# Attention products in 64-step blocks on quarters of TensorE, transposes in row halves, with waits through SyncE

## The chip, the cores and the metric

The kernel runs on one core of one Trainium2 chip. The metric is the device time of a launch in microseconds. Before the change three runs took 411.67, 411.74 and 412.81 us, with a median of 411.74 us.

## The reference

Two blocks follow each other. The first is linear attention with decay, for 4 batches, 8 heads, 768 steps and 48 numbers a head:

```python
for t in range(S):
    kt, vt, rt = (k[:, :, t], v[:, :, t], r[:, :, t])
    cur = np.einsum('bhd,bhe->bhde', u[None] * kt, vt)
    y[:, :, t] = np.einsum('bhd,bhde->bhe', rt, state + cur)
    state = w[None, :, :, None] * state + np.einsum('bhd,bhe->bhde', kt, vt)
```

So the output of step t takes in all earlier steps s < t, each decayed, and its own step s = t weighted with u instead. The second block is a mixture of eight experts over the 3072 rows of that output: a gate product gives logits, tokens are assigned greedily so that each expert has exactly 384, and each expert applies `relu(x @ w1) @ w2`. Everything is in 32-bit floats.

## The kernel before

The 768 steps are cut into 6 chunks of T = 128, and with 4 batches that gives 24 units, in the order of chunk and then batch. A unit holds all 8 heads, as 4 pairs a, with q = 0 or 1 for the head of a pair (j in the outputs). A head's 48 numbers lie in a field of PD = 64 partitions, so head q of a pair is on partitions 0 to 47 or 64 to 111.

The work of one unit n, with the names used below:

- `load(n)` (line 419) issues three transfers from SyncE's queue: kt, rt and vt of the unit, each 128 steps by 8 heads by 48 numbers, that is 1024 runs of 192 bytes. kt and rt have 6 buffers, vt has 8.
- `scale(n)` (line 432, VectorE) multiplies kt with powers of the decay into ks. `step_products(n)` (line 438, GpSimd) first calls `load(n + 4)` and then forms r*k*u, which `own(n)` (line 448, VectorE) sums into dd, one number per step and head.
- `rows_turned(n)` and `keys_turned(n)` (lines 456 and 468) transpose rt and ks on TensorE, four transposes of 128 by 128 each, into one bank of PSUM each. `receptances` (line 465, VectorE) and the copy of line 474 (ScalarE) bring them to rT and kT.
- `diagonal(n)` (line 451, ScalarE) writes eight matrices of 128 by 128 into AT, each the identity scaled with a head's dd.
- `pairs(n)` (line 517) forms the product of keys and receptances for each head, 8 matmuls, and VectorE copies it into AT where s < t (line 524), by a mask. AT[s, t] is then upper triangular with dd on its diagonal.
- `from_state(n)` (line 534), for all but the first chunk, and `outputs(n)` (line 560) add the share of the state and the share of AT into the same banks y_ps, and ScalarE copies them out (line 571). `new_state(n)` (line 543) forms the chunk's share of the state, for all but the last chunk.

The state and the outputs, y_ps, lie with their two halves of 64 columns on two halves of the partitions, so from_state already works in quarters of TensorE: 48 of 64 rows by 64 columns.

The loop over the units is at line 630. Iteration n transposes unit n + 2, loads unit n + 7 (through `step_products(n + 3)`), makes the pairs of n + 1 and the outputs of n. `logits` and `by_token` add the gate's logits of a chunk every fourth iteration. Pieces of the constants that the later search needs (`walk.constants`, line 755) are issued three to an iteration from iteration 3 on.

The order on every engine in the loop is written out by hand: two `manual_schedule` blocks (lines 620 and 621) hold TensorE, ScalarE, VectorE, GpSimd and SyncE to the order of the program. SyncE's queue has only the loads in the loop; it follows the program's order too, but it waits for other engines only where a buffer has to be free.

After the loop the attention's rows are transposed back, stored, and the search for the first expert's tokens runs (line 680). Then the experts follow (line 1439), bound by TensorE, with their weights on SyncE's queue.

## Time and profile before

| what | value |
|---|---|
| median of the runs | 411.74 us |
| the profiled execution | 412.36 us |
| its span, first to last instruction | 410.6 us |
| TensorE busy | 392.4 us, 96% |
| VectorE busy | 265.5 us, 65% |
| ScalarE busy | 148.3 us, 36% |
| GpSimd busy | 116.7 us, 28% |
| granted TensorE clock, mean | 0.998 |
| issue of a kt, rt, vt load to its landing, median | 4.6, 4.9, 4.9 us |
| ScalarE, one diagonal (line 454) | 391 ns, 192 times |
| VectorE, one masked copy of 512 elements (line 524) | 729 ns, 48 times |

PE is TensorE's matmuls and PEld its weight loads, DVE is VectorE, ACT is ScalarE, POOL is GpSimd and SPq is the queue of SyncE. L522 is line 522 of the kernel. A line of the timeline gives the start and the time from the first to the last end of a group of instructions, in us; the end of one group overlaps the start of the next, since matmuls are pipelined. A matmul in 32-bit floats shows as two records, a transpose as one.

### The profile page before, as it was taken

Reading aid. Unit: us, or ns where it says so; the run is one execution under the profiler, and the core shown is the slowest. Engines: PE = TensorE matmul, PEld = TensorE weight load, DVE = VectorE, ACT = ScalarE, POOL = GpSimd, SP = SyncE. Lnnn points to the kernel's source line nnn. Section 1 sums busy time; section 2 is a strip of 40 time slices with the busy share of each in tenths; the row PEclk is TensorE's granted clock in tenths of the full one; section 3 lists DMA queues with packets and bytes.
Section 4 is the critical chain, followed back from the end, with each engine's and each line's share of the span. In section 5 each row is a group of like instructions: output and inputs, shape, how many; then the busy total and the mean of one; then the engine's idle time right before and its main releaser. Section 6 shows DMA issues by size and latency. Waiting matters only on the chain. (4 is left out here: it accounts for less than half of the span.)

```text
span 410.6 us, 8511 instructions
## 1 busy us (share of the span) xinstructions
PE 392.4 (96%) x3174; PEld 289.7 (71%) x3174; DVE 265.5 (65%) x777; ACT 148.3 (36%) x382; POOL 116.7 (28%) x154
## 2 busy tenths in 40 slices
PE   7899999999987899989999999999999999999993
PEld 4688888888876585855785685595586577587583
DVE  5898879998568268478568658856856837421021
ACT  3898877878756021202112112121121211202200
POOL 5665965556200202210420320211112032201001
PEclk9999999999999999999999999999999999999999
DMA  9999999940029564712810730641461488201001
GB/s 146 166 169 175 176 161 173 176 81 2 3 96 335 176 231 160 228 38 63 294 68 5 277 121 23 208 178 39 172 214 40 142 306 285 57 21 38 0 21 38
DMA packets 93996, 54.43 MB, mean 133 GB/s; under 512 B 76784, under 2 KB 88176, under 8 KB 93936
## 3 DMA queue, kind: packets, MB, share of 16 engines
q1 hardware_dynamic: 89280, 41.70, 40.9%
q0 software_dynamic: 3072, 9.44, 6.9%
q10 hardware_dynamic: 1584, 2.56, 1.8%
q8 instruction: 29, 0.48, 0.5%
q14 instruction: 31, 0.25, 0.2%
HBM read 44.25 MB, written 9.44 MB: 131 GB/s over the span
## 5 line engine op out<-in xcount | busy, mean ns | idle before, releaser
L1328 PE MATMUL h_ps<-xT,w 128*128 128x384 f32 (+1 forms) x372 | 121.8, 475 | 0.0
L1328 PEld LDWEIGHTS h_ps<-xT,w 128*128 128x128 f32 x372 | 64.6, 190 | 35.9 <-issue 4.0
L1335 ACT ACTIVATE hid<-h_ps 128x384 f32<-128x384 f32 x56 | 27.5, 490 | 115.4 <-PE h_ps L1328 101.9
L1238 POOL DMA_INDIRECT xg<-x_rows,tok x24 | 25.0, 1040 | 144.0 <-issue 121.1
L454 ACT ACTIVATE AT<-ident,dd 128x128 f32<-128x128 f32 x192 | 59.4, 391 | 1.5 <-DVE dd L449 1.5
L1378 POOL DMA_INDIRECT out_dram<-o_sb,tok x24 | 25.9, 1078 | 106.1 <-DVE o_sb L1427 55.4
L1386 PE MATMUL o_ps<-w,hid 128*128 128x384 f32 x128 | 44.4, 493 | 0.9
L524 DVE COPY_PREDICATED AT<-mask,g_ps 128x512 f32<-128x512 uint8 x48 | 32.5, 729 | 7.2 <-PE g_ps L522 7.2
L1386 PEld LDWEIGHTS o_ps<-w,hid 128*128 128x128 f32 x128 | 23.5, 190 | 18.5 <-issue 4.4
L1407 PE MATMUL o_ps<-T,S 128*128 128x192 f32 x192 | 32.5, 326 | 0.0
L1407 PEld LDWEIGHTS o_ps<-T,S 128*128 128x128 f32 x192 | 31.4, 190 | 0.0
L522 PE MATMUL g_ps<-rT,kT 48*128 48x128 f32 x384 | 28.4, 285 | 0.1
L446 POOL TENSOR_TENSOR rk<-rk,u_bc 128x384 f32<-128x384 f32 x24 | 26.9, 1121 | 1.9
L445 POOL TENSOR_TENSOR rk<-rt,kt 128x384 f32<-128x384 f32 x24 | 24.8, 1034 | 9.0 <-DMA rt<-in_r_dram 7.0
L522 PEld LDWEIGHTS g_ps<-rT,kT 48*128 48x128 f32 x384 | 23.6, 187 | 4.9 <-issue 2.9
L567 PE MATMUL y_ps<-AT,vt 128*64 128x128 f32 x368 | 24.6, 276 | 0.0
L1407 PE MATMUL o_ps<-w,hid 128*128 128x192 f32 x128 | 24.6, 326 | 0.0
L1318 ACT COPY xT<-xT_ps 128x384 f32<-128x384 f32 x24 | 10.8, 481 | 34.2 <-PE xT_ps L1317 34.2
L1407 PEld LDWEIGHTS o_ps<-w,hid 128*128 128x128 f32 x128 | 20.9, 190 | 2.1
L1412 DVE TENSOR_TENSOR both<-o_ps,one 128x192 f32<-128x192 f32 x8 | 2.9, 358 | 27.7 <-ACT one L1418 27.7
L567 PEld LDWEIGHTS y_ps<-AT,vt 128*64 128x64 f32 x368 | 19.7, 137 | 0.9 <-issue 0.3
L466 DVE TENSOR_TENSOR rT<-rT_ps,wr 128x512 f32<-128x512 f32 x24 | 16.4, 683 | 5.3 <-PE rT_ps L461 5.2
(240 smaller groups left out, 593.1 us busy)
## 6 DMA issues: line engine op xcount, KB each, us to landing
w<-in_moe_w_dram SPq DMA_DIRECT2D x14, 1536.0 KB, 7.3
kt<-in_k_dram SPq DMA_DIRECT2D x24, 192.0 KB, 4.6
rt<-in_r_dram SPq DMA_DIRECT2D x24, 192.0 KB, 4.9
vt<-in_v_dram SPq DMA_DIRECT2D x24, 192.0 KB, 4.9
x_rows<-AT SPq DMA_DIRECT2D x8, 192.0 KB, 2.6
w<-in_moe_w_dram ACTq DMA_DIRECT2D x1, 1536.0 KB
x_rows<-rt SPq DMA_DIRECT2D x6, 192.0 KB, 3.4
x_rows<-ks SPq DMA_DIRECT2D x5, 192.0 KB, 2.8
```

Source lines behind the costliest of these rows:

```text
L445: nc.gpsimd.tensor_mul(rk, rt[:, :, 0:D], kt)
L446: nc.gpsimd.tensor_mul(rk, rk, self.u_bc.rearrange("p (h d) -> p h d", h=H))
L454: self.tc.nc.scalar.activation(AT[:, h % 2, h // 2, :], self.ident, AF.Copy, scale=dd[:, h:h + 1])
L522: nc.tensor.matmul(g_pss[q][:, a, :], kT[heads[q], a, :], rT[heads[q], a, :], start=True, stop=True)
L524: nc.vector.copy_predicated(out=AT[:, q], mask=mask.unsqueeze(1).to_broadcast([128, HP, T]), data=g_pss[q])
L567: nc.tensor.matmul(y[j][halves[i], g, :], vt[:, 2 * a + j, :], AT[:, j, a, :], start=(c == 0 and g == 0), stop=(g == 1), skip_group_check= ...
L1238: nc.gpsimd.indirect_dma_start(out=xg[:, c, :], out_offset=None, in_=x_dram, in_offset=bass.IndirectOffsetOnAxis(ap=tok[:, c:c + 1], axis=0))
L1328: product = nc.tensor.matmul(h_ps[:, cols], w1[:, f, ts(j, 128)], xT[:, f, cols], start=(f == 0), stop=(f == KD - 1))
L1335: nc.scalar.activation(hid[:, j, :], h_ps, AF.Relu)
L1378: nc.gpsimd.indirect_dma_start(out=out_rows[n * NC + c], out_offset=bass.IndirectOffsetOnAxis(ap=tok[:, c:c + 1], axis=0), in_=o_sb, in_of ...
L1386: nc.tensor.matmul(o_ps, hid[:, j, ts(c, 128)], w2[:, j, :], start=(j == 0), stop=(j == KF - 1))
L1407: nc.tensor.matmul(part, a[:, j, :], b[:, j, :], start=(j == 0), stop=(j == HF - 1))
```

## The change

Four parts, all but the last in the attention stage.

First, the products of pairs and outputs are cut into blocks of M = 64 steps. `pairs` makes two matmuls per head instead of one: block s = 0 against all 128 later steps, block s = 64 against the last 64 only. AT's rows 64 to 127 are stored with their columns moved to the left by 64, so that both diagonal blocks lie in columns 0 to 63: one masked copy serves both, and the block of rows 0 to 63 against steps 64 to 127 is copied whole by ScalarE (`across`). The diagonal matrices are 64 columns wide: five are made by ScalarE and three by one instruction of GpSimd. `outputs` takes the two row halves of AT and vt apart.

Second, the transposes of a unit are made in halves of 64 rows (`both_turned`): turn 0 takes rows 0 to 63 of rt and rows 64 to 127 of ks by turns, and turn 1 the other halves. In the same way outputs takes the heads j = turn for the first rows and the others for the last rows.

Third, [...] the first instructions of turn 1 wait until turn 0 has ended. `behind` makes that wait: a no-op on SyncE that waits for TensorE, and for which TensorE waits. The order of the loop changes with it: `scale` and `step_products` of n + 3, with the loads of n + 7, come first, pairs stands between the two turns of the transposes, and new_state between those of the outputs.

Fourth, eleven constants of the sure search (steps and top) are formed there and no longer ahead of it. The banks of PSUM in which the rows are turned at the end are three instead of four.

```diff
@@ -448,10 +453,14 @@
-    def diagonal(self, n, first=0, end=None):
+    def diagonal(self, n, part):
         AT, dd = self.live[n]["AT"], self.live[n]["dd"]
-        for h in range(first, end or self.r.shape[1]):
-            self.tc.nc.scalar.activation(AT[:, h % 2, h // 2, :], self.ident, AF.Copy, scale=dd[:, h:h + 1])
+        M, nc = T // 2, self.tc.nc
+        if part == 0:
+            nc.gpsimd.tensor_mul(AT[:, 1, 1:4, 0:M], self.own_step.unsqueeze(1).to_broadcast([128, 3, M]),
+                                 dd[:, 3::2].unsqueeze(2).to_broadcast([128, 3, M]))
+        for h in ((0, 1, 2), (4, 6))[part]:
+            nc.scalar.activation(AT[:, h % 2, h // 2, 0:M], self.own_step, AF.Copy, scale=dd[:, h:h + 1])
@@ -461,6 +470,32 @@
+    def behind(self, ins, other):
+
+        sync = mybir.DependencyInfo(mybir.DependencyClass.Sync, mybir.DependencyReason.DATA)
+        through = self.tc.nc.sync.nop().ins
+        self.tc.add_manual_dep(through, other.name, sync)
+        self.tc.add_manual_dep(ins, through.name, sync)
+
+    def both_turned(self, n, turn):
+
+        HP, live = self.r.shape[1] // 2, self.live[n]
+        names = ("rt", "rT_ps"), ("ks", "kT_ps")
+        if turn == 0:
+            for _, name in names:
+                live[name] = self.ps.tile([128, HP, T], F32, name=name)
+        for a in range(HP):
+            for i, (rows, into) in enumerate(names):
+                half = ts((turn + i) % 2, T // 2)
+                made = self.tc.nc.tensor.transpose(live[into][:, a, half],
+                                            live[rows][half, 2 * a:2 * a + 2, :].rearrange("p q d -> p (q d)"),
+                                            self.ident[half, half]).ins
+                if turn == 1 and a == 0:
+                    self.behind(made, live["half"])
+        live["half"] = made
+        if turn == 1:
+            self.tc.nc.scalar.copy(live["kT"], live.pop("kT_ps"))
@@ -518,10 +555,16 @@
         for a in range(HP):
-            for q in range(2):
-                nc.tensor.matmul(g_pss[q][:, a, :], kT[heads[q], a, :], rT[heads[q], a, :], start=True, stop=True)
-        for q in range(2):
-            nc.vector.copy_predicated(out=AT[:, q], mask=mask.unsqueeze(1).to_broadcast([128, HP, T]), data=g_pss[q])
+            for s in (0, M):
+                for q in range(2):
+                    nc.tensor.matmul(g_ps[s:s + M, q, a, 0:T - s], kT[heads[q], a, s:s + M], rT[heads[q], a, s:T],
+                                     start=True, stop=True)
+        for_all = mask.unsqueeze(1).unsqueeze(1).to_broadcast([128, 2, HP, M])
+        nc.vector.copy_predicated(out=AT[:, :, :, 0:M], mask=for_all, data=g_ps[:, :, :, 0:M])
+
+    def across(n):
+
+        nc.scalar.copy(live[n]["AT"][0:M, :, :, M:T], g_ps[0:M, :, :, M:T])
@@ -557,15 +600,24 @@
-        for g, j, i in order:
-            a = 2 * g + i
-            nc.tensor.matmul(y[j][halves[i], g, :], vt[:, 2 * a + j, :], AT[:, j, a, :],
-                             start=(c == 0 and g == 0), stop=(g == 1), skip_group_check=True)
+        for g in range(2):
+            for s in range(2):
+                j = (turn + s) % 2
+                for i in range(2):
+                    a, own = 2 * g + i, ts(s, M)
+                    made = nc.tensor.matmul(y[j][halves[i], g, s * M:T], vt[own, 2 * a + j, :], AT[own, j, a, 0:T - s * M],
+                                            start=(c == 0 and g == 0 and turn == 0), stop=(g == 1 and turn == 1),
+                                            skip_group_check=True).ins
+                    if turn == 1 and g == s == i == 0:
+                        mild.behind(made, live[n]["first"])
+        live[n]["first"] = made
+        if turn == 0:
+            return
@@ -625,29 +677,33 @@
             pairs(0)
-            mild.diagonal(1)
+            across(0)
+            for part in range(2):
+                mild.diagonal(1, part)
             mild.own(2)
             for n in range(N):
-                if n + 2 < N:
-                    mild.rows_turned(n + 2)
-                    mild.keys_turned(n + 2)
-                    mild.receptances(n + 2)
                 if n + 3 < N:
                     mild.scale(n + 3)
                     mild.step_products(n + 3)
                 if n + 2 < N:
-                    mild.diagonal(n + 2, 0, 4)
+                    mild.both_turned(n + 2, 0)
+                    mild.diagonal(n + 2, 0)
                 if n + 1 < N:
                     pairs(n + 1)
+                if n + 2 < N:
+                    mild.both_turned(n + 2, 1)
+                    mild.diagonal(n + 2, 1)
+                    mild.receptances(n + 2)
+                if n + 1 < N:
+                    across(n + 1)
                 if n > 0 and n % B == 0:
                     logits(n // B - 1)
-                if n + 2 < N:
-                    mild.diagonal(n + 2, 4)
                 from_state(n)
+                outputs(n, 0)
                 new_state(n)
                 if n > 0 and n % B == 0:
                     by_token(n // B - 1)
-                outputs(n)
+                outputs(n, 1)
@@ -662,7 +718,7 @@
-            banks += g_pss + [y_ps[:, 0], kv_ps]
+            banks += [g_ps[:, 0], kv_ps, y_ps[:, 0]]
```

More of the change, by code (lines that the diff above doesn't have):

```diff
@@ L343, in __init__ @@
         make_upper_triangular(nc, mask, val=1.0, diag=False)
-        self.mask = const.tile([128, 128], U8, name="mask")
-        nc.gpsimd.tensor_copy(self.mask, mask)
+        self.mask = const.tile([128, M], U8, name="mask")
+        self.own_step = const.tile([128, M], F32, name="own_step")
+        for i in range(2):
+            half = ts(i, M)
+            nc.gpsimd.tensor_copy(self.mask[half, :], mask[half, half])
+            nc.gpsimd.tensor_copy(self.own_step[half, :], ident[half, half])
         with part, tc.manual_schedule(engines={nc.tensor.engine, nc.vector.engine, nc.scalar.engine, nc.gpsimd.engine}):
@@ L408, in __init__ @@
             self.own(0)
-            self.diagonal(0, 0, 2)
+            self.diagonal(0, 0)
             self.keys_turned(0)
-            self.diagonal(0, 2)
+            self.diagonal(0, 1)
             self.step_products(1)
@@ L507, in attention_mild @@
     N = len(units)
+    M = T // 2
     lgT = {}
@@ L512, in attention_mild @@
     kv_ps = ps.tile([128, HP, T], F32, name="kv_ps")
-    g_pss = [ps.tile([128, HP, T], F32, name=f"g_ps{i}") for i in range(2)]
+    g_ps = ps.tile([128, 2, HP, T], F32, name="g_ps")
     last = []
@@ L558, in new_state, with outputs @@
                 nc.vector.tensor_mul(own, new, wc)
-    def outputs(n):
+    def outputs(n, turn):
         b, c = units[n]
@@ L564, in outputs @@
         y = banks_of(n)
-        for g, j, i in order:
-            a = 2 * g + i
-            nc.tensor.matmul(y[j][halves[i], g, :], vt[:, 2 * a + j, :], AT[:, j, a, :],
-                             start=(c == 0 and g == 0), stop=(g == 1), skip_group_check=True)
+        for g in range(2):
+            for s in range(2):
+                j = (turn + s) % 2
+                for i in range(2):
+                    a, own = 2 * g + i, ts(s, M)
[7 more added lines that the diff above has]
+            return
         into = turned[n].rearrange("p (g j) t -> p j g t", j=2)
@@ L676, in between @@
                 for _ in range(4):
-                    nc.tensor.matmul(g_pss[0][:, 0:3, :], ident, ident.unsqueeze(1).to_broadcast([128, 3, 128]),
+                    nc.tensor.matmul(g_ps[:, 0, 0:3, :], ident, ident.unsqueeze(1).to_broadcast([128, 3, 128]),
                                      start=True, stop=True)
@@ L743, in __init__ @@
         new("digits", [128, ND], I32)
-        new("steps", [128, 8, ND], I32)
-        new("top", [128, ND], I32)
         new("taken", [128, NT])
@@ L827, in constants @@
         nc.gpsimd.iota(self.digits, pattern=[[1, ND]], base=1, channel_multiplier=0)
-        yield
-        for g in range(8):
-            nc.vector.tensor_single_scalar(out=self.steps[:, g, :], in_=self.digits, scalar=28 - 4 * g,
-                                           op=ALU.logical_shift_left)
-            yield
-        nc.vector.tensor_single_scalar(out=self.top[:, 0:7], in_=self.steps[:, 0, 0:7], scalar=-1,
-                                       op=ALU.bitwise_xor)
-        yield
-        nc.vector.tensor_single_scalar(out=self.top[:, 7:ND - 1], in_=self.steps[:, 0, 7:ND - 1],
-                                       scalar=-2147483648, op=ALU.bitwise_xor)
-        yield
-        nc.vector.tensor_copy(self.top[:, ND - 1:ND], self.top[:, ND - 2:ND - 1])
         yield
@@ L1059, in surely @@
         tt(prop, self.by_expert(self.first_e), self.by_token(em), ALU.is_equal)
-        cand, bits = self.top, None
+        steps = pool.tile([128, 8, ND], I32, name="steps")
+        for g in range(8):
+            nc.vector.tensor_single_scalar(out=steps[:, g, :], in_=self.digits, scalar=28 - 4 * g,
+                                           op=ALU.logical_shift_left)
+        top = pool.tile([128, ND], I32, name="top")
+        nc.vector.tensor_single_scalar(out=top[:, 0:7], in_=steps[:, 0, 0:7], scalar=-1, op=ALU.bitwise_xor)
+        nc.vector.tensor_single_scalar(out=top[:, 7:ND - 1], in_=steps[:, 0, 7:ND - 1], scalar=-2147483648,
+                                       op=ALU.bitwise_xor)
+        nc.vector.tensor_copy(top[:, ND - 1:ND], top[:, ND - 2:ND - 1])
+        cand, bits = top, None
         for g in range(8):
@@ L1082, in surely @@
                 base = pool.tile([128, ND], I32, name="base")
-                tt(base, self.steps[:, g + 1, :], flip.to_broadcast([128, ND]), ALU.bitwise_xor)
+                tt(base, steps[:, g + 1, :], flip.to_broadcast([128, ND]), ALU.bitwise_xor)
                 cand = pool.tile([128, ND], I32, name="cand")
```

## The prediction

> **What bounds the kernel now.** First the busy shares: is one engine full?

> ```profile
> PE 392.4 (96%) x3174; PEld 289.7 (71%) x3174; DVE 265.5 (65%) x777; ACT 148.3 (36%) x382; POOL 116.7 (28%) x154
> ```

> TensorE is. The change touches only the attention stage, 16.4 to 115.7 us of the span, so the second view is TensorE's own timeline there: iteration 0 of the loop (line 630), then iteration 11.

> ```profile
> 16.44 0.66 PE L461 MATMUL rT_ps<-ident,rt 128*128 128x128 f32 x4
> 16.94 0.60 PE L472 MATMUL kT_ps<-ident,ks 128*128 128x128 f32 x4
> 17.47 1.71 PE L522 MATMUL g_ps<-rT,kT 48*128 48x128 f32 x16
> 19.11 0.56 PE L550 MATMUL kv_ps<-vt,ks 128*48 128x48 f32 x16
> 19.50 1.06 PE L567 MATMUL y_ps<-AT,vt 128*64 128x128 f32 x16
> 20.49 0.66 PE L461 MATMUL rT_ps<-ident,rt 128*128 128x128 f32 x4
> ...
> 62.49 0.66 PE L461 MATMUL rT_ps<-ident,rt 128*128 128x128 f32 x4
> 62.98 0.60 PE L472 MATMUL kT_ps<-ident,ks 128*128 128x128 f32 x4
> 63.51 1.16 PE L522 MATMUL g_ps<-rT,kT 48*128 48x128 f32 x16
> 64.60 0.67 PE L540 MATMUL y_ps<-rT,state 48*64 48x128 f32 x16
> 65.20 0.56 PE L550 MATMUL kv_ps<-vt,ks 128*48 128x48 f32 x16
> 65.60 1.06 PE L567 MATMUL y_ps<-AT,vt 128*64 128x128 f32 x16
> 66.59 0.66 PE L461 MATMUL rT_ps<-ident,rt 128*128 128x128 f32 x4
> ```

> Each group begins where the one before ends: a unit costs 66.59 - 62.49 = 4.10 us of TensorE (3.50 us for the first four, which have no state, line 540), and nothing else ends a wait. From start to start: transposes 1.02, pairs 1.09, from_state 0.60, kv 0.40, outputs 0.99.

> Third, the queue that the new waits go through. SyncE issues the loads of line 426 in program order; unit 7's are the last three before 28.99:

> ```profile
> 23.70 0.37 SPq L426 DMA_DIRECT2D kt<-in_k_dram  x1
> 24.23 0.46 SPq L426 DMA_DIRECT2D rt<-in_r_dram  x1
> 24.81 0.78 SPq L426 DMA_DIRECT2D vt<-in_v_dram  x1
> 25.77 0.84 SPq L426 DMA_DIRECT2D kt<-in_k_dram  x1
> 26.78 0.92 SPq L426 DMA_DIRECT2D rt<-in_r_dram  x1
> 27.81 1.00 SPq L426 DMA_DIRECT2D vt<-in_v_dram  x1
> 28.99 1.65 SPq L426 DMA_DIRECT2D kt<-in_k_dram  x1
> ```

> One issue holds SyncE for 0.4 to 2.7 us, one after the other, since the DMA engines are full there:

> ```profile
> DMA  9999999940029564712810730641461488201001
> ```

> By the program, unit 7 is loaded in iteration 0 (line 637 loads n + 3 + 4). TensorE began iteration 0 at 16.44; SyncE is done with that load at 28.81. SyncE is 12 us behind the program, and in the kernel before nobody minds, as iteration 0 itself needs only unit 3. The last load is issued at 84.5 and iteration 16 starts at 84.38: only there has TensorE come level.

> [...] within a mode a wave of records starts 0.109 us after the one before (two records in pairs and outputs, four 7 ns apart in from_state, line 540); at each change of mode the next group starts 0.20 us after the last record and its first wave takes 0.15 to 0.21. A change so costs (1.02 - 0.87) to (1.09 - 0.89), about 0.16 us. [...] The granted clock stays full 3.6 us past the last matmul (403.9), to 409.0, and averages 0.52 over 409.0 to 410.6; a pause within the kernel isn't shown.

> **The change, part by part,** per unit of TensorE.

> - *Pairs.* 8 products become 16 in four quarters. The column quarter of block s=0 still gets 4 heads x 2 records of 128 columns: 8 waves x 0.109 = 0.87 as now. The omitted block lay in the other quarter, which only idles sooner. I take 1.06 with one change of mode. Bounds: 1.31 + 0.16 if 64-column records don't overlap 128-column ones; 0.67 + 0.16 if the saved quarter of work shortens the group.
> - *Outputs.* The same: each row half s=0 does 4 products x 2 records of 128 columns, 2 x 4 waves x 0.109 = 0.87. Same two-sided bounds, +0.44 and -0.22.
> - *Transposes.* 8 waves of 128 columns become 8 waves of two halves with 64 columns, 2 x 4 x 0.055 = 0.44 in place of 0.87. No row has this form; the weight load of a transpose takes 140 ns where a 128-column product's takes 188, so loading shouldn't hold the wave. Bounds: 0.44, or 0.87 if it does.
> - *Modes.* Per unit turn 0, pairs, turn 1, from_state with outputs 0, kv, outputs 1: six changes for four, +0.32.
> - Sum with state: 0.38 + 1.06 + 0.38 + (0.436 + 0.436 + 0.16) + (0.36 + 0.16) + (0.436 + 0.16) = 3.97 for 4.10, **-0.13**, 16 units: -2.1. Without state 3.54 for 3.50: +0.2 for four. The last four have no kv between the two halves of outputs, so that wait is open (below): +0.25 in all after the modes saved.
> - *ScalarE* per unit: 2.44 us of diagonals becomes five of 64 columns plus a 512-element copy, some 1.3 + 0.58. *VectorE*: one predicated copy of 0.73 for two. *GpSimd*: one more of some 0.5 (a product of the same 192 elements, line 556, takes 0.507), to 2.8 in a unit of 3.97. All hidden under TensorE, which waits for none of them; if uncovered, at most GpSimd's 0.5 a unit. Moving the search's 11 constants: VectorE only, under the loop, 0; three more small GpSimd copies ahead of the loop fall into its idle 3.0 us before 6.83. Three banks for four at the end: rows' copies take 0.48 and their transposes 0.44, so 0.
> - *Waits through SyncE.* Turn 1's first transposes and the first product of outputs 1 wait for no-ops on SyncE. Queued behind them on TensorE is everything; behind them on SyncE, the loads of unit n + 8. Price with SyncE free: end of a record 0.27 after its start, hop 0.1 (kT's copy starts 0.09 after the transposes' end), 0.05, hop 0.1, so 0.52 after the last record. Outputs 1 has kv in front (start at +0.71): hidden; open without kv, +0.35. Turn 1 has pairs in front (+1.26): hidden.

> But SyncE isn't free. In iteration 0 the order there is: three issues of unit 7, then turn 1's no-op. Nothing lets those issues come earlier; they run against full DMA engines from 1.7 us on. So the no-op runs at 28.81 + 0.1, turn 1 at 29.05. Without the wait: 16.44 + 0.38, pairs from 17.4 (VectorE must free g_ps) to 18.5. **TensorE stands still for 10.5 us**, and iteration 1 starts at 29.05 + 0.38 + 0.60 + 0.52 + 0.60 = 31.15 for 20.49: **+10.7**.

> It isn't caught up: TensorE has no idle time later. [...] Later the no-op of outputs(n) releases unit n + 8's loads, and the next turn 1 waits for their issue. After outputs 0 ends, SyncE needs 0.2 + three issues of 1.7 (12.99 to 14.67[...]) to 1.9 + 0.15, about 2.2; TensorE has 0.52 + 0.60 + 0.38 + 1.06 less 0.07, 2.5, before it comes to turn 1. It just fits; in iterations 1 to 3 the DMA needs 3.4 a unit (24 in 82), +0.5 in all, and issues of up to 2.7 will sometimes stick out, **+1** (0 to 8).

> Sum: 10.7 + 1.7 + 0.2 + 0.5 - 2.1 + 0.25 + 1 = 12.2, rounded to **+12**: the span 410.6 becomes 422.6. That execution took 412.4, 0.6 above the median; laid on the median 411.74, **423.7 us**.

> **The rivals.**

> 1. *Stall, and TensorE dearer.* Mixed column counts don't overlap (+0.88 a unit), or half-row transposes save nothing (+0.43 on 22, +9.5), or SyncE sticks out by 0.5 on 16 units (+8). For: none of these forms is in the trace, and the vt issues reach 2.68. Against: from_state overlaps four. 429 to 445, about 433.
> 2. *The change does what it says:* products really get shorter by the missing quarter, 0.44 x 24 = -10.6. Against: the busy quarter keeps its columns. With the stall 413.1.
> 3. *No stall.* One mechanism: SyncE is at the first no-op when TensorE gets there, at 18.5 rather than 28.9. Then only the sums: -2.1 + 0.2 + 0.25 = -1.6, 410.1, faster. It decides once SyncE arrives before about 19.5 (stall under 1, no half clock). For: iteration 0 needs nothing of unit 7, so any other order of that queue gives it. Against: the queue is filled in program order, and its issues follow kt, rt, vt, unit by unit throughout.

> **How the numbers follow.** Main 0.52 (418 to 429), rival 1 0.25, rival 2 0.07, rival 3 0.16. Range 413 to 440: all of the main case, most of rival 1 and half of rival 2. Within 0.3% (1.2 us, what a measurement of this kernel can tell) are parts of rivals 2 and 3: faster 0.11, same 0.05, slower 0.84.

> **What would show it.** Right: a gap on TensorE before turn 1 in iteration 0, ended by SyncE near 29 us; then units of about 4.0; pairs still 1.06, transposes 0.38 per turn. Wrong: no such gap, or units of 3.5 or less (rival 2), or of 4.4 and more with turn 1 waiting for SyncE (rival 1). The forecast fails if the no-ops are queued ahead of the loads.

## The result, and the profile after

The changed kernel takes 429.41 us (median of 4 runs, 428.24 to 429.95) against 412.27 us (411.67 to 415.41) for the kernel before, run beside it. The ratio is 1.0396, with a 95% interval of 1.0338 to 1.0454: 17.1 us slower, where the forecast was 12 us slower (423.7 us, with a range of 413 to 440). The profiled execution took 429.95 us, its span is 428.2 us and its mean granted clock 0.959.

From the page of the changed kernel: the busy shares, the granted clock in 40 slices of 10.7 us, and a row of the costliest groups (busy time, mean ns of one, then the idle time before it and what ended it).

```profile
PE 398.8 (93%) x4118; PEld 291.6 (68%) x4118; DVE 245.3 (57%) x742; ACT 132.9 (31%) x334; POOL 130.7 (31%) x181
...
PEclk9955599999999999999999999999999999999999
...
L491 PE MATMUL rT_ps<-ident,rt 64*128 64x64 f32 x176 | 22.2, 253 | 9.1 <-SPq L477 9.1
```

TensorE is busy for 6.4 us more although it is given less to do: that is no sign of heavier work, since the clock row has three slices at half speed, from about 21 to 54 us. The third line has the idle time that was forecast: the first transposes of turn 1 (line 491) wait 9.1 us in all, and SyncE's no-op of line 477 ends all of it. TensorE's timeline of the same kernel shows where, in iteration 0:

```profile
16.62 1.09 PE L560 MATMUL g_ps<-rT,kT 48*64 48x128 f32 x32 [1.14 <-ACT AT L567]
...
26.37 0.36 PE L491 MATMUL rT_ps<-ident,rt 64*128 64x64 f32 x1 [8.66 <-SPq L477]
...
30.57 1.97 PE L560 MATMUL g_ps<-rT,kT 48*64 48x128 f32 x32
```

Pairs end at 17.71, turn 1 starts at 26.37, and in brackets stands the 8.66 us of idle time between. (The 1.14 us ahead of pairs are a wait for ScalarE's copy of line 567.) Before the gap a pairs group takes 1.09 us, after it 1.97. SyncE's own queue in that stretch:

```profile
25.64 0.63 SPq L431 DMA_DIRECT2D vt<-in_v_dram  x1
28.45 0.37 SPq L431 DMA_DIRECT2D kt<-in_k_dram  x1
```

The issue of unit 7's last transfer ends at 26.27, and turn 1 runs 0.10 us later. The next load is issued only from 28.45, after the second no-op of the iteration.

The busy time by stretches (PE, PEld, DVE, ACT, POOL, each with its count, then the granted clock, the DMA share and GB/s) has the second half of the story:

```profile
17.70:26.40 8.70, 0.04 (x3) 0.03 (x1) 0.73 (x1) 0.79 (x4) 3.21 (x4) 0.67 0.96 188
26.40:54.80 28.40, 28.40 (x456) 22.41 (x456) 11.02 (x21) 13.18 (x37) 9.12 (x13) 0.50 0.52 102
```

After the gap TensorE works for 28.4 us without a pause, and all that time at half its clock. In the clock's records the low stretch lies from 20.70 to 54.83. Then one unit, from the start of its pairs to the next one's, looks like this:

```profile
60.59 1.09 PE L560 MATMUL g_ps<-rT,kT 48*64 48x128 f32 x32
...
63.02 0.56 PE L593 MATMUL kv_ps<-vt,ks 128*48 128x48 f32 x16
63.52 0.65 PE L613 MATMUL y_ps<-AT,vt 64*64 64x128 f32 x16
...
64.50 1.09 PE L560 MATMUL g_ps<-rT,kT 48*64 48x128 f32 x32
```

A unit takes 64.50 - 60.59 = 3.91 us, where it took 4.10; kv, between the two halves of outputs, has 63.52 - 63.02 = 0.50. The 17 us by stretches of the two profiled executions, measured between starts of the kv products (lines 550 and 593) of the units named, and to the start of the search's most_ps product at the end of the stage:

| stretch | before | after | difference | what it is |
|---|---|---|---|---|
| start to unit 0 | 19.11 | 28.09 | +8.98 | gap 8.66; half clock 0.81; pairs' wait for ScalarE, less the earlier start of the loop (15.01 for 16.44), -0.5 |
| units 0 to 4 | 15.61 | 26.86 | +11.25 | half clock |
| units 4 to 19 | 66.08 | 63.41 | -2.67 | cheaper units, with one stop of 0.46 for SyncE |
| unit 19 to most_ps | 12.84 | 12.04 | -0.80 | last units |

The sum is +16.76, of 17.6 between the two spans. The same four units take 15.33 us in the next experiment, which keeps the full clock, so the half clock costs 26.86 - 15.33 = 11.53 there. From the end of the gap to the first kv product it is 28.09 - 26.37 = 1.72 us, where that experiment has 0.91 from the end of pairs: 0.81 more. Together that is **12.3 us**: more than the gap that set it off. (Texts below that were written before their runs say 12.5.)

### The profile page after: what moved, and what is told of

Read it like the earlier page. It is cut to its first block, busy times and chain, and to the rows that moved or that the text cites. A ratio compares the mean times of both kernels' runs of the same rounds, so it can differ in the third digit from the quotient of the medians.

```text
span 428.2 us, 10342 instructions
## 1 busy us (share of the span) xinstructions
PE 398.8 (93%) x4118; PEld 291.6 (68%) x4118; DVE 245.3 (57%) x742; ACT 132.9 (31%) x334; POOL 130.7 (31%) x181
## 5 line engine op out<-in xcount | busy, mean ns | idle before, releaser
L1438 PEld LDWEIGHTS o_ps<-w,hid 128*128 128x128 f32 x128 | 23.5, 190 | 18.5 <-issue 4.4
L463 ACT ACTIVATE AT<-own_step,dd 128x64 f32<-128x64 f32 x120 | 33.7, 342 | 1.5 <-DVE dd L454 1.5
L613 PE MATMUL y_ps<-AT,vt 64*64 64x128 f32 (+1 forms) x736 | 33.3, 274 | 0.3
L563 DVE COPY_PREDICATED AT<-mask,g_ps 128x512 f32<-128x512 uint8 x24 | 17.7, 738 | 23.0 <-PE g_ps L560 14.4
L560 PE MATMUL g_ps<-rT,kT 48*64 48x128 f32 (+1 forms) x768 | 29.7, 275 | 1.1 <-ACT AT L567 1.1
L491 PE MATMUL rT_ps<-ident,rt 64*128 64x64 f32 x176 | 22.2, 253 | 9.1 <-SPq L477 9.1
L491 PEld LDWEIGHTS rT_ps<-ident,rt 64*128 64x128 f32 x176 | 15.8, 152 | 18.2 <-SPq L477 10.4
L450 POOL TENSOR_TENSOR rk<-rt,kt 128x384 f32<-128x384 f32 x24 | 26.3, 1095 | 0.1
L560 PEld LDWEIGHTS g_ps<-rT,kT 48*64 48x64 f32 x768 | 23.3, 146 | 3.8 <-ACT AT L567 1.3
L613 PEld LDWEIGHTS y_ps<-AT,vt 64*64 64x64 f32 x736 | 22.9, 149 | 2.8 <-SPq L477 0.8
L491 PE MATMUL kT_ps<-ident,ks 64*128 64x64 f32 x176 | 22.2, 253 | 0.0
```

The lines of the kernel that those rows point to most:

```text
L450: nc.gpsimd.tensor_mul(rk, rt[:, :, 0:D], kt)
L463: nc.scalar.activation(AT[:, h % 2, h // 2, 0:M], self.own_step, AF.Copy, scale=dd[:, h:h + 1])
L491: made = self.tc.nc.tensor.transpose(live[into][:, a, half], live[rows][half, 2 * a:2 * a + 2, :].rearrange("p q d -> p (q d)"), self.iden ...
L560: nc.tensor.matmul(g_ps[s:s + M, q, a, 0:T - s], kT[heads[q], a, s:s + M], rT[heads[q], a, s:T], start=True, stop=True)
L613: made = nc.tensor.matmul(y[j][halves[i], g, s * M:T], vt[own, 2 * a + j, :], AT[own, j, a, 0:T - s * M], start=(c == 0 and g == 0 and tur ...
L1438: nc.tensor.matmul(o_ps, hid[:, j, ts(c, 128)], w2[:, j, :], start=(j == 0), stop=(j == KF - 1))
```

## The experiments

The theory after the result: SyncE's place in its queue makes the gap, the gap lowers the clock, and without a gap the change itself is a small gain. The rivals: the new forms keep the clock low by themselves; a gap on TensorE always costs that much; blocks or halves alone carry the loss or the gain.

**The waits through ScalarE.** ScalarE's queue has no loads. Its no-op stands right behind turn 0 and behind the first half of outputs, and what ScalarE does in between is put behind it.

```diff
-        through = self.tc.nc.sync.nop().ins
+        through = self.tc.nc.scalar.nop().ins
 ...
                     mild.both_turned(n + 2, 1)
-                    mild.diagonal(n + 2, 1)
                     mild.receptances(n + 2)
-                if n + 1 < N:
-                    across(n + 1)
 ...
                 outputs(n, 0)
+                if n + 2 < N:
+                    mild.diagonal(n + 2, 1)
+                if n + 1 < N:
+                    across(n + 1)
                 new_state(n)
```

> The changed kernel, with the same waits led through ScalarE instead of SyncE (two of ScalarE's steps move behind the wait of the outputs), so that no wait stands behind a load's issue. Theory (order of SyncE's queue, then the halved clock): the 8.7 us gap in iteration 0 and the half clock to 54.8 us both vanish; units stay at 3.9 us and 3.4 us without state; 429.4 - 8.7 - 12.5 = about 408, between 406 and 411. Rival (the quarter and half-row forms of the work are what costs): no less than 420, since they are all still there.

Measured: 408.35 us (three executions, 408.18 to 409.93) against 411.62, ratio 0.992 (0.99 to 0.9939). TensorE's timeline in iteration 0, and the stretch from 20 to 60 us:

```profile
18.09 1.09 PE L563 MATMUL g_ps<-rT,kT 48*64 48x128 f32 x32 [1.15 <-ACT AT L570]
...
21.56 1.09 PE L563 MATMUL g_ps<-rT,kT 48*64 48x128 f32 x32
```

```profile
20.00:60.00 40.00, 40.00 (x1136) 32.40 (x1136) 28.64 (x57) 29.92 (x83) 32.14 (x53) 1.00 0.93 184
```

From pairs to pairs it is 3.47 us, with no gap between, and the clock stays at 1.00. So in these executions the whole loss belongs to the queue that the waits go through: all the rest of the change is a gain of 3.3 us. The parts add up: 408.35 + 8.66 + 12.3 = 429.3, and 429.41 was measured. And in this trace the new forms don't lower a clock that is full.

A fourth execution took 420.42 us, at a mean granted clock of 0.963 where the three have 0.996 to 0.997. Its trace isn't kept. The 12 us and the mean clock are like those of the next experiment, where 27.3 us of half clock cost 11.6 us (mean clock 0.965). So this kernel may have lost the clock there too, with no load ahead of its waits; that isn't shown.

**The load moved nearer, waits still through SyncE.** In iteration 0 the no-op then stands behind unit 5's load and not unit 7's.

```diff
-        self.load(n + 4)
+        self.load(n + 2) if n > 1 else None
```

> The changed kernel with its waits on SyncE, but each load called two units later (n + 2 instead of n + 4), so that in iteration 0 the first wait stands behind unit 5's load and not unit 7's. Theory: the wait is reached when unit 5 is issued, 20.5 us in the changed kernel's trace, so the gap shrinks from 8.7 to about 2.9 us; [...] about 429.4 - 5.8 - 12.5 = 411, up to 416 if loads then come late. If the gap shrinks but the clock is halved all the same: about 423. Rival (forms of the work): 429, the gap being a by-product.

Measured: 423.64 us, ratio 1.0295 (1.0266 to 1.0323). TensorE's timeline and one stretch:

```profile
20.69 0.37 PE L491 MATMUL rT_ps<-ident,rt 64*128 64x64 f32 x1 [3.04 <-SPq L477]
```

```profile
36.00:48.00 12.00, 12.00 (x196) 9.30 (x194) 4.60 (x9) 5.95 (x17) 3.77 (x7) 0.50 0.51 100
```

The gap shrinks as expected, to 3.04 us, and 12 us are lost all the same, since even that gap halves the clock: it falls at 20.61 and comes back at 47.91. By the units at half clock (6.05 us for 3.47) these 27.3 us are worth an estimated 27.3 x (1 - 3.47 / 6.05) = 11.6. My belief that such a gap is just too short to count was wrong.

**The gap filled with work.** The no-op stays late, but 13 products of 128 x 384 run in the gap.

```diff
                     pairs(n + 1)
+                if n == 0:
+                    for _ in range(13):
+                        nc.tensor.matmul(kv_ps[:, 0:3, :], ident, ident.unsqueeze(1).to_broadcast([128, 3, 128]),
+                                         start=True, stop=True)
                 if n + 2 < N:
                     mild.both_turned(n + 2, 1)
```

> The changed kernel with 13 extra matmuls of 128x384 (8.5 us) on TensorE in iteration 0, ahead of the second turn of transposes, into a bank nobody reads: the wait stays as it is, but TensorE works through it. Theory (the clock falls to half in the gap and its slow recovery costs 12.5 us): the clock stays full, 429.4 - 12.5 = about 417, 415 to 419. Rival (time after the gap is set by SyncE and the loads, not by the clock): 426 to 430.

Measured: 420.6 us (418.91 to 423.18), ratio 1.0221 (1.0172 to 1.0271). The clock is full from 20 to 60 us, and its mean in the profiled execution is 0.996:

```profile
20.00:60.00 40.00, 38.39 (x874) 28.89 (x876) 20.62 (x42) 22.20 (x63) 23.28 (x39) 1.00 0.73 144
```

That is 429.41 - 420.6 = 8.8 us less than the changed kernel, with the wait still there. The time is above the 415 to 419 that were expected, for two reasons that its trace shows: the loop began 1.5 us later than in the changed kernel's execution, and TensorE's later stops for SyncE are 0.25, 0.96, 0.26 and 0.23 us, where the changed kernel has one of 0.46. With these 2.7 us counted in, the clock is worth an estimated 11.5 us by this road, against the 12.3 of the table.

**The kernel before with one such wait.** Nothing of the change but this: the first pair product of iteration 0 waits behind the load of unit 7.

```diff
+                if n == 1 and a == q == 0:
+                    sync = mybir.DependencyInfo(mybir.DependencyClass.Sync, mybir.DependencyReason.DATA)
+                    through = nc.sync.nop().ins
+                    tc.add_manual_dep(through, mild.turned_last.name, sync)
+                    tc.add_manual_dep(made.ins, through.name, sync)
```

> The kernel before with one wait of the same kind only: the first pair product of iteration 0 waits for a no-op on SyncE behind unit 7's load. Nothing else is changed. Theory: TensorE stands still from 17.5 to about 29, 11.4 us. If the clock then returns[...]: 412 + 11.4 + 1.7 = 425. If it stays half until the first logits, as in the changed kernel, four units of 3.5 and part of the fifth take double: 412 + 11.4 + 14 = 437. Rival (slow recovery is a trait of the new forms): 425.

Measured: 424.32 us, ratio 1.0312 (1.0287 to 1.0337). TensorE's timeline, then the stretches after the gap:

```profile
27.83 2.08 PE L522 MATMUL g_ps<-rT,kT 48*128 48x128 f32 x16 [9.93 <-SPq L525]
```

```profile
28.00:32.00 4.00, 4.00 (x46) 3.78 (x48) 2.02 (x4) 0.00 (x0) 0.00 (x0) 0.50 1.46 182
32.00:36.00 4.00, 4.00 (x52) 3.32 (x50) 1.73 (x4) 2.24 (x6) 2.01 (x2) 0.75 0.74 135
```

The gap is 1.3 us longer than in the changed kernel, but the full clock is back at 34.02, 6.2 us after work resumes. Half of 6.2 on top of 9.93 makes 13.0, and 12.7 were measured. A pause of 10 us does therefore not cost 28 us of half clock by itself: with the old forms the clock is back after 6. So in the changed kernel something in the new forms keeps it low.

**Which of the new forms?** One kernel has the half-row transposes alone and their wait through SyncE, the other the blocks alone, with whole transposes and the outputs' wait through SyncE.

```diff
 (the kernel before)
-                    mild.rows_turned(n + 2)
-                    mild.keys_turned(n + 2)
 ...
+                    mild.both_turned(n + 2, 0)
                     mild.diagonal(n + 2, 0, 4)
                 if n + 1 < N:
                     pairs(n + 1)
+                if n + 2 < N:
+                    mild.both_turned(n + 2, 1)
+                    mild.receptances(n + 2)
 (the kernel after)
-                    mild.both_turned(n + 2, 0)
+                    mild.rows_turned(n + 2)
+                    mild.keys_turned(n + 2)
+                    mild.receptances(n + 2)
 ...
-                    mild.both_turned(n + 2, 1)
                     mild.diagonal(n + 2, 1)
-                    mild.receptances(n + 2)
```

> The kernel before with the transposes alone changed (row halves in two turns, pairs between them, the wait through SyncE behind unit 7's load); pairs, outputs and diagonals as before. The gap in iteration 0 (about 9 us) and the fall of the clock are expected under every theory. What keeps the clock at half afterwards in the changed kernel? If the half-row transposes do: half until the first logits, 27 us after the gap and more, about 424 to 427. If the products in quarters do: full again within 7 us as in the kernel before with one wait, about 419 to 422.

> The changed kernel with whole transposes, as before the change; pairs and outputs in quarters, and the wait of the outputs through SyncE behind unit 7's load. A gap of about 7 us in iteration 0 under every theory. If the products in quarters keep the clock at half: half until the first logits near 55 us, about 428 to 432. If the half-row transposes do: full again within 7 us, about 420.

Measured, in two executions each: halves alone 418.64 us, ratio 1.0169 (1.0116 to 1.0223), blocks alone 419.01 us, ratio 1.0178 (1.0122 to 1.0234). The gaps are 9.3 and 5.7 us. Two stretches of the first, then the same of the second:

```profile
28.00:32.00 4.00, 3.77 (x50) 3.33 (x50) 1.98 (x4) 2.04 (x6) 1.25 (x1) 0.50 1.46 186
32.00:36.00 4.00, 3.53 (x74) 3.23 (x72) 2.67 (x6) 3.72 (x11) 1.00 (x1) 0.96 0.93 164
```

```profile
28.00:32.00 4.00, 4.00 (x87) 3.27 (x86) 2.12 (x5) 2.67 (x8) 0.00 (x0) 0.81 0.66 133
32.00:36.00 4.00, 4.00 (x94) 3.36 (x92) 3.07 (x7) 3.24 (x9) 3.09 (x4) 1.00 0.89 173
```

Neither keeps the clock low: it is back at 32.31 and 29.54, 4.1 and 4.0 us after work resumes. Both expectations had put the blame on one form or the other, and both fell. Only the two together, in the changed kernel and in the one with the load moved, stay at half clock, for 28.4 and 27.2 us of unbroken work. In both of these the first logits (128 x 32 products on all rows, 1.93 us) run just ahead of the return: they start at 51.23 and 45.56, and the clock is back at 54.83 and 47.91. The first from_state follows them (from 53.10 and 47.42).

**A burst right after the gap.** In the changed kernel seven products of 128 x 384 follow turn 1 in iteration 0.

```diff
+                if n == 0:
+                    for _ in range(7):
+                        nc.tensor.matmul(kv_ps[:, 0:3, :], ident, ident.unsqueeze(1).to_broadcast([128, 3, 128]),
+                                         start=True, stop=True)
                 if n > 0 and n % B == 0:
                     logits(n // B - 1)
```

> The changed kernel with seven extra matmuls of 128x384 in iteration 0, right after the gap. Theory (the kind of work keeps the clock low, not the time): full clock within 4 to 7 us of the gap's end; the burst costs about 6 to 7 us, the rest of the 12.5 us comes back: 423 to 425. Rival (the clock needs its time whatever runs): half until 54.8 us still, with 9 us more to do: 438.

Measured, in two executions: 425.07 us, ratio 1.0308 (1.023 to 1.0386), 4.3 us less than the changed kernel although it does more; 1.3 of them are a shorter gap (7.37 us in its trace). The stretch in which the burst ends:

```profile
28.00:32.00 4.00, 4.00 (x9) 2.25 (x8) 0.00 (x0) 0.00 (x0) 0.00 (x0) 0.61 0.00 0
```

The clock is full from 31.09 on, 5.8 us after the gap, where it took 28. So here the kind of work, and not the time since the gap alone, brought it back; what it is about that work isn't shown.

**Each part alone, waits through ScalarE.** No gap and no low clock here: these two price the parts themselves. The edits are those of the two kernels above, with the waits of the first experiment.

> The kernel before with the transposes alone changed, the wait through ScalarE, so without the gap. The prediction's sum gives transposes 0.43 us less in waves, and no change of mode between them and pairs, which have the same shape of tile: TensorE needs some 3.6 us a unit in place of 4.1. Theory A (TensorE sets the pace): 20 to 22 units x 0.5, 401 to 403. Theory B (VectorE, at 3.8 to 4.1 us a unit before, and ScalarE at 3.6 take over): 408 to 411, with waits of pairs or transposes on VectorE or ScalarE.

> The changed kernel with whole transposes, the wait of the outputs through ScalarE, so without the gap: the blocks alone. Prediction's sum (the busy quarter keeps its columns, nothing is saved but changes of mode): transposes 1.02 + pairs 1.02 + from_state 0.49 + outputs 0.54 + kv 0.49 + outputs 0.58 = 4.1 us a unit as before, 410 to 413. Rival (the missing block shortens the products, 0.44 a unit): about 401.

Measured: halves alone 406.8 us, ratio 0.9879 (0.9839 to 0.9918); blocks alone 411.22 us, ratio 0.9991 (0.9978 to 1.0004). Halves are the gain, and blocks are none that the time shows. From halves alone, one unit of TensorE's timeline:

```profile
69.93 1.11 PE L548 MATMUL g_ps<-rT,kT 48*128 48x128 f32 x16
...
73.50 1.11 PE L548 MATMUL g_ps<-rT,kT 48*128 48x128 f32 x16
```

3.57 us: 0.53 less than before, and 0.34 less than with blocks on top. But not all units reach it. The stretch from 60 to 90 us, first of the kernel before and then of halves alone, and a line of the waits of halves alone (total us, count, longest):

```profile
60.00:90.00 30.00, 30.00 (x559) 25.00 (x556) 29.07 (x59) 24.13 (x71) 16.49 (x23) 1.00 0.96 157
60.00:90.00 30.00, 27.98 (x626) 24.15 (x626) 29.66 (x64) 24.68 (x72) 19.52 (x24) 1.00 0.94 160
```

```profile
PEld rT_ps L480 <- DVE rT L492: 7.3, 16, 1.0
```

VectorE, nearly full already before, is busy for 29.66 of 30 us and TensorE, which had no idle time there, waits for it: the bound has moved. That is why the time fell between the two expectations. The same stretch with blocks alone:

```profile
60.00:90.00 30.00, 30.00 (x776) 25.07 (x769) 22.24 (x45) 20.40 (x56) 22.70 (x32) 1.00 0.63 124
```

Here VectorE has 22.24 us: the blocks take a quarter of VectorE's work away. For TensorE they do little: a unit with state takes 3.99 us for 4.10, one without 3.56 for 3.50.

**Halves, and eleven constants moved.** If VectorE holds the halves back, its extra work in the loop should matter. The fourth part of the change (constants formed in the search) is added to halves alone.

```diff
-        for g in range(8):
-            nc.vector.tensor_single_scalar(out=self.steps[:, g, :], in_=self.digits, scalar=28 - 4 * g,
-                                           op=ALU.logical_shift_left)
-            yield
 ...
+        steps = pool.tile([128, 8, ND], I32, name="steps")
+        for g in range(8):
+            nc.vector.tensor_single_scalar(out=steps[:, g, :], in_=self.digits, scalar=28 - 4 * g,
+                                           op=ALU.logical_shift_left)
```

> As e7_turns_scalar (half-row transposes alone, the wait through ScalarE), and the eleven constants of the sure search moved out of the loop as in the change. If VectorE sets the pace of iterations 4 to 17 there (29.7 us busy of 30 between 60 and 90 us), its 11 instructions of some 0.39 us come off the path: 406.8 - 2 to 4 = 403 to 405. If another engine or TensorE sets it: 406.8.

Measured: 405.93 us against 411.57, ratio 0.9845 (0.9788 to 0.9902), the best of all kernels here. In its stretch from 60 to 90 us VectorE has slack again:

```profile
60.00:90.00 30.00, 29.43 (x662) 25.67 (x662) 26.68 (x55) 25.65 (x76) 21.12 (x27) 1.00 0.58 114
```

In that stretch two units are still longer than their like (4.35 us for 3.57, 5.22 for 4.58), where halves alone has four. The time is above the 403 to 405 that were expected. The 0.9 us to the kernel without the moved constants is inside the intervals of both, so the gain of this step is not settled; the relief of VectorE (29.66 to 26.68) is.

**Steps in the order of TensorE's modes.** A mode is the shape of the pieces of the array that a group of instructions takes. With blocks each unit has six changes of mode. This order (turn 0, kv, turn 1, from_state, outputs 0, pairs, outputs 1, waits through ScalarE) has fewer.

```diff
                     mild.both_turned(n + 2, 0)
                     mild.diagonal(n + 2, 0)
-                if n + 1 < N:
-                    pairs(n + 1)
+                new_products(n)
                 if n + 2 < N:
                     mild.both_turned(n + 2, 1)
 ...
                 outputs(n, 0)
                 new_state(n)
 ...
+                    if not (ends and n + 2 < N):
+                        pairs(n + 1)
+                    across(n + 1)
+                outputs(n, 1)
```

> As e1_wait_scalar (all parts of the change, waits through ScalarE), with the steps of a unit ordered by TensorE's shapes: transposes, the state's product, transposes, then from_state, first outputs, pairs and last outputs, all in quarters. Four changes of shape a unit for six. Theory (a change of shape costs 0.1 to 0.16): 3.6 to 3.7 us for 3.9 on 20 units, 403 to 405. Rival (ScalarE's queue, which now has the wait of the first turn behind a copy, holds TensorE 0.1 to 0.3 a unit): 407 to 411.

Measured: 412.53 us, ratio 1.0029 (0.9998 to 1.0059). The waits show one reason:

```profile
PEld y_ps L586 <- ACT xT L630: 6.2, 13, 1.2
```

from_state now comes before ScalarE has copied the unit before out of y_ps; with that wait (6.2 us over 13 units) most units take 4.03 us, where 3.6 to 3.7 were expected. What the modes alone would give isn't shown.

## Why the prediction was right, and where it was off

- **The order of SyncE's queue: right.** The gap before turn 1 in iteration 0 is there, and SyncE ends it. It is 8.66 us for 10.5, as the no-op ran near 26.3 rather than 28.9: the loads were issued earlier in that execution than in that of the kernel before. The waits through ScalarE remove it. Whether turn 1 has to wait at all isn't shown: no run leaves the waits out.
- **Half clock, +1.7: the step that was mis-sized.** It cost 12.3 us. The 1.7 in the sum stands for the time at half clock after the pause, and no trace showed it: in that of the kernel before the clock falls once, 5.2 us after the last matmul. In the runs the full clock is back 4.0 to 6.2 us after work resumes with the old forms, with either new one among them, or where dense products follow, and 28.4 us after with both new forms. That more than explains the excess of the total: 12.2 + 10.6 - 1.8 for the shorter gap would be 21.0, and 16.8 is left by the units (about -1.9), SyncE's later issues (-0.8), the tail (-1.1) and the start of the loop (-0.5). That the time still fell into the range is so in part luck: a term seven times too small was offset in part by some 6 us in which the other terms came out lower than forecast. The kernel's own forms had not been seen after a pause. The prediction's line on the end of the trace was misread too: from the last matmul (403.9) to 409.1 are 5.2 us, not 3.6.
- **Cost of a unit, 3.97: right within 0.07.** Measured 3.91 with state (-0.19 for -0.13) and 3.47 without (for 3.54). Pairs take 1.02 (1.06 forecast), a turn of transposes 0.39 (0.38), kv 0.50 (0.52), the second outputs 0.58 (0.60). So the weight load doesn't hold the half-row transposes (a turn at 0.44 + 0.16 = 0.60 would have shown that), and records of 64 and 128 columns do overlap (without that, pairs would have taken 1.31 + 0.16 = 1.47).
- **The omitted block saves TensorE nothing: right.** Blocks alone are at 0.9991, and their unit is 0.11 us shorter, where shorter products would have made it 0.44. On top of halves they even cost 3.91 - 3.57 = 0.34 a unit. Changes of mode may be the reason; no run shows that alone.
- **VectorE at nothing: wrong, without harm here.** I read its 65% of the span as slack. In the loop it was busy for 29.07 of 30 us (60 to 90) already before, and 23.26 in the changed kernel. It is what limits halves alone. ScalarE isn't wholly hidden either: in iteration 0 pairs wait 1.14 us for its copy of line 567.
- **Later issues of SyncE, +1 and +0.5:** one stop of 0.46 us, and 0.7 in all over units 4 to 19 against the waits through ScalarE (63.41 for 62.68). **Tail, +0.25:** it came out at -0.80; which of its parts gained was not looked into.
- **The rivals.** The one with a dearer TensorE gives nearly the measured time (429 to 445), for none of its reasons: no form was dearer at full clock. Shorter products are refuted by blocks alone. No stall, forecast at 410.1, is what the waits through ScalarE bring: 408.35, but for the one execution of 420.42.

## What to carry to other kernels

A wait through another engine's queue waits for everything that is queued ahead there (8.66 us here, behind unit 7's loads): give it a queue that has come level with the waiting engine, not one that runs behind and is not missed. In these runs a pause of TensorE cost itself and then the clock's return, and the return depended on the work that followed: 4.0 to 6.2 us in four kernels, 28.4 and 27.2 in the two with both new forms and nothing dense behind the gap. After a pause that can't be helped, try dense full-array products first, as in the burst (back after 5.8 us). The changed kernel's small pieces ran well on a full clock (3.91 us a unit for 4.10) and still left a halved one low for 28.4 us. When a stage is shortened on its bounding engine, read the other engines' share of that stage, not of the span.
